# Chunked delta rule ahead of a routed feed-forward: the substitution looks one row ahead, V is scaled into PSUM, T lies in runs of 32, and two banks are read as one

## The chip, the core and the metric

The kernel runs on one NeuronCore of a Trainium2 chip. The metric is the time of one execution on the device in microseconds; lower is better. TensorE (PE) multiplies and transposes, VectorE (DVE) and ScalarE (ACT) work element by element on SBUF and PSUM, GpSimd (POOL) and SyncE (SP) mostly issue DMAs. Each engine runs its instructions in the order in which they stand; between engines, and between instructions of VectorE that depend on each other, semaphores make one wait for another.

## The reference

```python
# attention: B=4, H=8, S=768, D=48
k_n = k / (norm(k) + 1e-6)
state = zeros(B, H, D, D)
for t in range(S):
    y[:, :, t] = q[:, :, t] @ state
    v_old = k_n[:, :, t] @ state
    state += beta_t * outer(k_n[:, :, t], v[:, :, t] - v_old)
x = y.transpose(0, 2, 1, 3).reshape(B * S, H * D)      # 3072 x 384
# feed-forward: 8 experts of 384 -> 1024 -> 384
e = token_ids * 2654435761 % 8
out[e == i] = relu(x[e == i] @ w1[i]) @ w2[i]
```

All of it is in f32.

## The kernel before

The sequence is cut into 24 chunks of 32 tokens (C = 32, NU = 24), in 6 groups of 4 (GC, NG). Batch and token of the chunk lie on the 128 partitions (4 x 32), the 8 heads in the free dimension. Within a chunk the recurrence is solved in closed form. The products of keys with keys and queries with keys ("gram", L358) give a triangular system per head; its inverse T is found on VectorE by substitution; and then the chunk needs the following steps, written by `chunk(c)`:

- *ask*: keys and queries times the state S (L502, TensorE), into bank A (keys) and bank Y (queries).
- R = V1 − A (L525, VectorE, two halves). V1 is V times a factor per token (`scale_v`, L424, VectorE).
- *solve*: T times R into bank B (L536), 32 matmuls of 64x64 weights; the weights are read out of the tile Tz, in which T for two halves of the partitions lies with zeros between.
- W, a copy of bank B (L546, ScalarE, two halves).
- *update*: keys times W, added to the state in `psS` (L557); S is copied out by ScalarE (L632, two copies), for the last chunks the second one by VectorE (L630).
- *answer*: W with the masked query products MT (L584) on top of bank Y; `x_sb` is the copy of Y (L592), which GpSimd scatters to `x_scratch` in DRAM (L597).

Beside these steps a chunk prepares one that comes 8 or 9 later: *turn* transposes Q and K on TensorE (L321, into bank A for Q, Z and B for K) and ScalarE copies them to KQ (L330); *gram* goes into banks Z and B, and from there GK (keys with keys, L373, ScalarE) and GQ (queries with keys times a mask, L382, VectorE). ScalarE makes MT from GQ (L400). Chunks 0 and 2 do a second turn and gram, and the preparation ends with chunk 13.

One inverse serves a group of four chunks. VectorE transposes the keys' products (L439), and then runs 31 steps of two ops each, a product of the rows found so far with one column of the system (`tmp`, L476) and its addition to the rows left (U, L474):

```python
for j in range(C - 1):
    task("DVE", ns, (f"U{i}", row), ("tmp",), lambda j=j: step(j, False))
    task("DVE", ns, ("tmp",), (f"U{i}",), lambda j=j: step(j, True))
```

Last, a 128x1024 transpose puts T into TU (L485), and `spread_t` copies TU into Tz, by ScalarE for the first two groups (L410), by four DMAs of GpSimd's queue with runs of 4 KB for the others (L417).

The order of the work on each engine is written out: every step is a `task` with an engine, an estimated duration and names that it reads and writes, and `order()` runs through all tasks once and gives each engine the ready task with the longest rest of a chain behind it. TensorE and SyncE keep the order in which the tasks are made. LAG holds the estimated delay from one engine to the next, and a task may be put behind another that will soon be ready, within .35 of its own duration.

Then x is read back sorted by expert, and the feed-forward follows on TensorE (L993, L1023). The many small operations that count tokens per expert (`routing`) run on VectorE in the attention's time.

## Time and profile before

| what | us |
|---|---|
| median of 3 runs | 544.59 (543.64 to 547.6) |
| the profiled execution | 547.66 |
| its span, first to last instruction | 546.1 |
| TensorE busy | 474.7 (87%) |
| VectorE busy | 265.9 (49%) |
| ScalarE busy | 152.8 (28%) |
| GpSimd busy | 148.6 (27%) |
| first solve starts | 51.45 |
| second solve starts | 68.36 |
| solve of chunk 14 starts, the first without preparation | 194.58 |
| last solve starts | 265.76 |
| the experts' work begins and ends | 280.68, 538.33 |

A chunk's period is told here from one solve's start to the next. The shares are those of the whole span; the stages have different limits, so the busy times of the stretches between these marks say more than they do. 1.56 us of the profiled execution lie outside the span. The clock columns show how much of TensorE's full rate was granted, as a share of 2.4 GHz.

### The profile page before, as it was taken

Reading aid. Unit: us, or ns where it says so; the run is one execution under the profiler, and the core shown is the slowest. Engines: PE = TensorE matmul, PEld = TensorE weight load, DVE = VectorE, ACT = ScalarE, POOL = GpSimd, SP = SyncE. Lnnn points to the kernel's source line nnn. Section 1 sums busy time; section 2 is a strip of 40 time slices with the busy share of each in tenths; the row PEclk is TensorE's granted clock in tenths of the full one; section 3 lists DMA queues with packets and bytes.
Section 4 is the critical chain, followed back from the end, with each engine's and each line's share of the span. In section 5 each row is a group of like instructions: output and inputs, shape, how many; then the busy total and the mean of one; then the engine's idle time right before and its main releaser. Section 6 shows DMA issues by size and latency. Waiting matters only on the chain. (4 is left out here: it accounts for less than half of the span.)

```text
span 546.1 us, 16071 instructions
## 1 busy us (share of the span) xinstructions
PE 474.7 (87%) x6756; PEld 357.2 (65%) x6756; DVE 265.9 (49%) x764; ACT 152.8 (28%) x353; POOL 148.6 (27%) x195
## 2 busy tenths in 40 slices
PE   4874697998999888768549999999999999999993
PEld 3754586887888777667425756657576676768651
DVE  8799889899878989942111311212121221212100
ACT  3633666666455544523201000010100001010100
POOL 9400000013021032121100045071623517070621
PEclk9875878799678787988859999999999999999997
DMA  6745554446442132290099190451808145010000
GB/s 127 126 80 128 101 96 90 81 103 126 94 102 60 36 87 54 57 295 33 32 232 331 50 297 29 126 190 26 286 15 256 63 116 199 4 37 5 30 25 27
DMA packets 104345, 58.03 MB, mean 106 GB/s; under 512 B 90902, under 2 KB 99553, under 8 KB 103376
## 3 DMA queue, kind: packets, MB, share of 16 engines
q1 hardware_dynamic: 94000, 43.40, 31.9%
q0 software_dynamic: 5888, 12.53, 7.1%
q10 hardware_dynamic: 4384, 1.06, 1.1%
q8 instruction: 54, 0.88, 0.7%
q14 instruction: 19, 0.16, 0.1%
HBM read 44.51 MB, written 10.65 MB: 101 GB/s over the span
## 5 line engine op out<-in xcount | busy, mean ns | idle before, releaser
L993 PE MATMUL h_ps<-xT,w_sb 128*128 128x424 f32 (+3 forms) x384 | 130.3, 500 | 11.3 <-DMA xr<-x_scratch 11.3
L1030 POOL DMA_INDIRECT out_dram<-o_sb,idx x90 | 87.3, 970 | 160.4 <-DVE o_sb L1025 119.3
L993 PEld LDWEIGHTS h_ps<-xT,w_sb 128*128 128x128 f32 x384 | 74.3, 194 | 65.4 <-issue 28.1
L1023 PE MATMUL o_ps<-h_sb,w_sb 128*128 128x424 f32 (+3 forms) x336 | 112.3, 494 | 0.0
L1023 PEld LDWEIGHTS o_ps<-h_sb,w_sb 128*128 128x128 f32 x336 | 84.4, 251 | 27.2 <-issue 0.3
L996 ACT ACTIVATE h_sb<-h_ps 128x424 f32<-128x424 f32 (+3 forms) x32 | 15.9, 496 | 233.9 <-PE h_ps L993 209.0
L998 DVE TENSOR_SCALAR h_sb<-h_ps 128x424 f32<-128x424 f32 (+3 forms) x32 | 18.1, 565 | 113.5 <-PE h_ps L993 97.1
L597 POOL DMA_INDIRECT x_scratch<-x_sb,slot x24 | 25.1, 1047 | 160.0 <-ACT MT L400 93.5
L474 DVE TENSOR_TENSOR U<-U,tmp 128x31 f32<-128x31 f32 (+15 forms) x186 | 63.9, 343 | 5.8
L476 DVE TENSOR_TENSOR tmp<-U,Ni 128x31 f32<-128x31 f32 (+15 forms) x186 | 63.5, 342 | 5.5
L502 PE MATMUL bank<-S,KQ 128*32 128x96 f32 x1472 | 44.4, 277 | 13.4 <-ACT x_sb L592 5.2
L536 PE MATMUL bank<-R,Tz 64*64 64x48 f32 x736 | 46.3, 279 | 10.5 <-DVE R L525 7.0
L1025 DVE STREAM_TRANSPOSE o_sb<-o_ps 128x384 f32<-128x384 f32 (+2 forms) x21 | 15.5, 740 | 80.1 <-PE o_ps L1023 80.1
L536 PEld LDWEIGHTS bank<-R,Tz 64*64 64x64 f32 x736 | 43.2, 200 | 15.5 <-ACT GK L373 5.9
L502 PEld LDWEIGHTS bank<-S,KQ 128*32 128x32 f32 x1472 | 36.8, 125 | 17.8 <-ACT x_sb L592 6.5
L632 ACT ACTIVATE S<-psS 48x768 f32<-48x768 f32 x43 | 34.6, 805 | 20.7 <-PE psS L557 20.2
L557 PE MATMUL psS<-W,K 32*112 32x96 f32 x736 | 30.0, 313 | 4.9 <-ACT W L546 3.9
L584 PE MATMUL bank<-W,MT 64*64 64x48 f32 x768 | 32.1, 241 | 0.5 <-ACT W L546 0.5
L584 PEld LDWEIGHTS bank<-W,MT 64*64 64x64 f32 x768 | 28.9, 156 | 4.7 <-issue 3.4
L557 PEld LDWEIGHTS psS<-W,K 32*112 32x112 f32 x736 | 25.6, 214 | 9.2 <-ACT W L546 8.0
L330 ACT ACTIVATE KQ<-bank 128x256 f32<-128x256 f32 (+1 forms) x55 | 26.6, 487 | 16.8 <-DVE GQ L382 8.1
L546 ACT ACTIVATE W<-bank 128x192 f32<-128x192 f32 x48 | 13.2, 328 | 60.2 <-PE bank L536 57.4
(123 smaller groups left out, 403.2 us busy)
## 6 DMA issues: line engine op xcount, KB each, us to landing
w_sb<-in_moe_w_dram SPq DMA_DIRECT2D x14, 1536.0 KB
K<-in_k_dram SPq DMA_DIRECT2D x92, 48.0 KB
Q<-in_q_dram SPq DMA_DIRECT2D x88, 48.0 KB
V<-in_v_dram SPq DMA_DIRECT2D x80, 48.0 KB
xr<-x_scratch SPq DMA_DIRECT2D x16, 145.5 KB
Tz<-TU POOLq DMA_DIRECT2D x16, 128.0 KB
w_sb<-in_moe_w_dram SPq DMA_DIRECT2D x3, 512.0 KB
w_sb<-in_moe_w_dram SPq DMA_DIRECT2D x4, 384.0 KB
```

What stands on the lines that cost most here:

```text
L330: lambda bank=bank, at=at, us=us, m=m: nc.scalar.activation(KQ[:, us[0]:us[0] + m, a, :], bank[:, at:at + P * m].rearrange("p (u x) -> p u ...
L474: nc.vector.tensor_tensor(U[:, n:, 0:n], U[:, n:, 0:n], t, op=ALU.add)
L476: nc.vector.tensor_tensor(t, U[:, j:n, 0:n].to_broadcast([P, m, n]), Ni[:, j, n:, None].to_broadcast([P, m, n]), op=ALU.mult)
L502: nc.tensor.matmul(res[quarter(b), u], lhsT=KQ[:, u, a, quarter(b)], rhs=S0[:, b, u].rearrange("p r d -> p (r d)"), start=(u == 0), stop=True,
L536: nc.tensor.matmul(pw[rows, h], lhsT=Tz[rows, :, :, x0 + h].rearrange("p e i -> p (e i)"), rhs=R[rows, h], start=(h == 0), stop=True, skip ...
L557: nc.tensor.matmul(psS[0][0:DP + D, b, 2 * D * u:2 * D * u + 2 * D], lhsT=K4[quarter(b), u].rearrange("p r d -> p (r d)")[:, 0:DP + D], rh ...
L584: nc.tensor.matmul(py[rows, h], lhsT=MT[rows, h].rearrange("p e i -> p (e i)"), rhs=W[rows, h], start=(c == 0 and h == 0), stop=True, skip ...
L597: put = nc.gpsimd.indirect_dma_start(out=x_dram[:, :], out_offset=bass.IndirectOffsetOnAxis(ap=slot[:, c:c + 1], axis=0), in_=x_sb.rearran ...
L632: nc.scalar.activation(S1[half(r), :, :, r], new[half(r), :, :, r], ACT.Copy)
L993: nc.tensor.matmul(h_ps[:, :width], lhsT=w1_sb[:, co, fo * P:(fo + 1) * P], rhs=xT[:, co, :width], start=(co == 0), stop=(co == CO - 1))
L1023: nc.tensor.matmul(os_ps[i][:, 0:width], lhsT=w2_sb[:, fo, i::CO], rhs=h_sb[:, fo, 0:width], start=(fo == 0), stop=(fo == FO - 1))
L1030: scat = nc.gpsimd.indirect_dma_start(out=out_q, out_offset=bass.IndirectOffsetOnAxis(ap=idx[e][:, k:k + 1], axis=0), in_=o_sb[:, k], in_o ...
```

## The change

- **Look-ahead.** A step of the substitution is three ops in place of two: the product for the rows beyond the next (L511), the next row by itself in one op (`row`, L507), and the addition for the rows beyond it (L515). The product of step j+1 needs the row of step j, and not its addition. There are two `Ni` and four `tmp`.
- **V and R.** `scale_v` writes its product into bank A (L447), and the keys' ask adds to it there (`start=False` for the keys); W is copied with a factor of −1, so the state in `psS` is negative, and so is the sign of x_sb's copy. R is then a copy of bank A by ScalarE (L574): one of 128x384 in the chunks up to 13, two halves after. W likewise (L596). There are two R, and no V1. One matmul with zeros (L918) opens bank A.
- **T in runs.** Tz and TU hold the 32 elements of a row of T side by side, so the solve (L585) reads 64 weights in a row. The transpose into TU writes with a stride (L535). The first chunk of each group goes to Tz by ScalarE (L434), as do all four in the first two groups; the other three chunks by GpSimd's DMAs, in runs of 128 bytes.
- **Pairs.** Banks Z and B are one tile, `pair`. The copy GK (L384), the mask GQ (L388) and the copy of the turned keys (L341) are one op each on both. The turn of Q goes into bank Z.
- **Order.** Estimated durations and delays are other numbers (LAG of ScalarE 90 for 85, of VectorE 122 for 65; ops of the substitution are not put behind a coming task, but for those of the first one, for which the share is 2.0). The answer stands ahead of the turn of K. The last part of the routing's small operations is made after the last inverse (`routing_tail`).

```diff
-        bank_z, bank_a, bank_b, bank_y = tiles(4, "bank", [P, BANK], ps)
+        bank_a, bank_y = tiles(2, "bank", [P, BANK], ps)
+        pair = ps.tile([P, 2, BANK], F32, name="pair")
+        bank_z, bank_b = pair[:, 0], pair[:, 1]
...
-        Tzs = tiles(2, "Tz", [P, 2, C, NX])
-        TUs = tiles(2, "TU", [P, C, NX])
+        Tzs = tiles(2, "Tz", [P, NX, 2, C])
+        TUs = tiles(2, "TU", [P, NX, C])
...
-        LAG = {"PE": 255, "ACT": 85, "DVE": 65, "POOL": 150, "SP": 0}
+        LAG = {"PE": 255, "ACT": 90, "DVE": 122, "POOL": 150, "SP": 0}
...
+            def wait_for(i):
+                return {"inv": 0.0, "inv0": 2.0}.get(tasks[i]["kind"], 0.35)
...
+                if paired:
+                    task("ACT", 500, names, (f"GK{g % 3}{cc}0", f"GK{g % 3}{cc}1"),
+                         lambda: nc.scalar.activation(
+                             GK[:, :, cc].rearrange("p j u r -> p r u j"), both[:, :, :, 0],
+                             ACT.Copy))
+                    task("DVE", 340, names, (f"GQ{c % NGQ}0", f"GQ{c % NGQ}1"),
+                         lambda: nc.vector.tensor_tensor(
+                             GQ.rearrange("p u r y -> p r u y"), both[:, :, :, 1],
+                             mask[:, None, None, :].to_broadcast([P, 2, HU, C]),
+                             op=ALU.mult), boost=4000)
+                    return
...
+            near = GC if g < 2 else 1
+            for cc in range(near):
+                xs_ = slice(H * cc, H * cc + H)
+                for e in range(2):
+                    task("ACT", 450, (f"TU{g % 2}",), (f"Tz{g % 2}{cc}{e}", f"Tz{g % 2}{cc}{e}+"),
+                         lambda e=e, xs_=xs_: nc.scalar.activation(
+                             Tz[:, xs_, e], TU[:, xs_], ACT.Copy, scale=kmask[:, e:e + 1]))
+            for b in range(B if near < GC else 0):
+                x0 = H * near
+                task("POOL", 800, (f"TU{g % 2}",),
+                     [f"Tz{g % 2}{cc}{b % 2}" + "+" * (b // 2) for cc in range(near, GC)],
+                     lambda b=b, x0=x0: nc.gpsimd.dma_start(
+                         out=Tz[quarter(b), x0:, b % 2], in_=TU[quarter(b), x0:]), kb=150)
...
+            task("DVE", 470, four(f"v{c % 4}_") + (f"ntok{g % 3}",), ("A",),
+                 lambda: nc.vector.tensor_tensor(
+                     bank_a[:, 0:H * D].rearrange("p (h d) -> p h d", h=H), Vs[c % 4],
+                     n[:, :, None].to_broadcast([P, H, D]), op=ALU.mult))
...
+            def ahead(j, what):
+                n, m = j + 1, C - 2 - j
+                t = tmps[2 * i + j % 2][:, 0:n * m].rearrange("p (m n) -> p m n", n=n)
+                if what == "row":
+                    nc.vector.scalar_tensor_tensor(
+                        out=U[:, n, 0:n], in0=U[:, j, 0:n], scalar=Ni[:, j, n:n + 1],
+                        in1=U[:, n, 0:n], op0=ALU.mult, op1=ALU.add)
+                elif what == "mult":
+                    nc.vector.tensor_tensor(t, U[:, j:n, 0:n].to_broadcast([P, m, n]),
+                                            Ni[:, j, n + 1:, None].to_broadcast([P, m, n]),
+                                            op=ALU.mult)
+                else:
+                    nc.vector.tensor_tensor(U[:, n + 1:, 0:n], U[:, n + 1:, 0:n], t, op=ALU.add)
...
-            task("DVE", 1200, (f"U{i}",), (f"TU{i}",), lambda: nc.vector.transpose(
-                TUs[i], U))
+            task("DVE", 1860, (f"U{i}",) + (tuple(rows) if g in EAGER else ()), (f"TU{i}",), lambda: nc.vector.transpose(
+                TUs[i].rearrange("p x i -> p i x"), U))
...
-                                     start=(u == 0), stop=True,
+                                     start=(a == 1 and u == 0), stop=True,
...
+            for hs in ((range(H),) if busy else hheads):
+                part = slice(D * hs.start, D * hs.stop)
+                task("ACT", 490 if busy else 305, ("A",), [f"R{c % 2}{x}" for x in range(2)
+                                              if hheads[x].start in hs],
+                     lambda part=part: nc.scalar.activation(
+                         R.rearrange("p h d -> p (h d)")[:, part], flat_a[:, part], ACT.Copy))
...
-                        nc.tensor.matmul(pw[rows, h], lhsT=Tz[rows, :, :, x0 + h].rearrange("p e i -> p (e i)"),
+                        nc.tensor.matmul(pw[rows, h], lhsT=Tz[rows, x0 + h].rearrange("p e i -> p (e i)"),
...
-                         W[:, hs.start:hs.stop], pw[:, hs.start:hs.stop], ACT.Copy))
+                         W[:, hs.start:hs.stop], pw[:, hs.start:hs.stop], ACT.Copy, scale=-1.0))
...
-                turn(turned, 1, [("A", bank_a, 0, range(HU))])
+                turn(turned, 1, [("Z", bank_z, 0, range(HU))])
```

The first place is TensorE in one chunk with preparation, from the turn of K to the next one's products. In the names, `bank_161` is Z, `bank_162` A, `bank_163` B and `bank_164` Y; after, `bank_164` is A and `bank_165` Y. Before:

```order
L321 MATMUL bank_161<-ident,K_80 128x128 x2
L321 MATMUL bank_163<-ident,K_80 128x128 x2
L584 MATMUL bank_164<-W_107,MT_138 64x48 x16
L502 MATMUL bank_162<-S_97,KQ_116 32x96 x16
L502 MATMUL bank_164<-S_97,KQ_116 32x96 x16
L536 MATMUL bank_163<-R_105,Tz_140 64x48 x16
L321 MATMUL bank_162<-ident,Q_94 128x128 x4
L557 MATMUL psS<-W_106,K_84 112x96 x16
L358 MATMUL bank_161<-KQ_114 32x64 x4
L358 MATMUL bank_163<-KQ_114 32x64 x4
```

After:

```order
L632 MATMUL bank_165<-W_106,MT_137 64x48 x16
L331 MATMUL pair<-ident,K_84 128x128 x4
L552 MATMUL bank_164<-S_97,KQ_119 32x96 x16
L552 MATMUL bank_165<-S_97,KQ_119 32x96 x16
L585 MATMUL pair<-R_103,Tz_138 64x48 x16
L331 MATMUL pair<-ident,Q_93 128x128 x4
L607 MATMUL psS<-W_105,K_88 112x96 x16
L368 MATMUL pair<-KQ_117 32x64 x32
L632 MATMUL bank_165<-W_105,MT_136 64x48 x16
L331 MATMUL pair<-ident,K_85 128x128 x4
```

The answer has moved ahead of the turn of K, the solve's weights come from the new Tz, and the products go to the pair in one piece of 32 matmuls where before they went to the two banks in turns of 4.

The second place is VectorE in the middle of a substitution. Before, with the masks of two banks, R and a V product among the steps:

```order
L474 TENSOR_TENSOR U_148<-U_148,tmp 128x15x17
L476 TENSOR_TENSOR tmp<-U_148,Ni 128x252
L382 TENSOR_TENSOR GQ_135<-bank_163,mask 128x4x32
L382 TENSOR_TENSOR GQ_135<-bank_161,mask 128x4x32
L474 TENSOR_TENSOR U_148<-U_148,tmp 128x14x18
L476 TENSOR_TENSOR tmp<-U_148,Ni 128x247
L474 TENSOR_TENSOR U_148<-U_148,tmp 128x13x19
L476 TENSOR_TENSOR tmp<-U_148,Ni 128x240
L525 TENSOR_TENSOR R_105<-V_103,bank_162 128x192 x2
L474 TENSOR_TENSOR U_148<-U_148,tmp 128x12x20
L424 TENSOR_TENSOR V_104<-V_102,ntok_143 128x384
L476 TENSOR_TENSOR tmp<-U_148,Ni 128x231
```

After, with one mask and a V product into bank A:

```order
L507 SCALAR_TENSOR_TENSOR U_147<-U_147,Ni_149 128x13
L515 TENSOR_TENSOR U_147<-U_147,tmp_152 128x18x13
L511 TENSOR_TENSOR tmp_153<-U_147,Ni_149 128x238
L388 TENSOR_TENSOR GQ_133<-pair,mask 128x2x4x32
L507 SCALAR_TENSOR_TENSOR U_147<-U_147,Ni_149 128x14
L515 TENSOR_TENSOR U_147<-U_147,tmp_153 128x17x14
L511 TENSOR_TENSOR tmp_152<-U_147,Ni_149 128x240
L507 SCALAR_TENSOR_TENSOR U_147<-U_147,Ni_149 128x15
L515 TENSOR_TENSOR U_147<-U_147,tmp_152 128x16x15
L511 TENSOR_TENSOR tmp_153<-U_147,Ni_149 128x240
L447 TENSOR_TENSOR bank_164<-V_101,ntok_142 128x384
L507 SCALAR_TENSOR_TENSOR U_147<-U_147,Ni_149 128x16
```

A step has become three ops, in which `tmp` changes between two tiles and no op reads what the one just ahead of it wrote; R is gone from this engine.

The third place is ScalarE over one chunk with preparation. Before:

```order
L400 ACTIVATE MT_138<-GQ_128,kmask 128x8x32 x2
L546 ACTIVATE W_106<-bank_163 128x192 x2
L330 ACTIVATE KQ_110<-bank_162 128x4x128
L632 ACTIVATE S_98<-psS 48x16x48 x2
L330 ACTIVATE KQ_110<-bank_161 128x2x128
L330 ACTIVATE KQ_110<-bank_163 128x2x128
L373 ACTIVATE GK_124<-bank_161 128x4x32
L373 ACTIVATE GK_124<-bank_163 128x4x32
L592 ACTIVATE x_sb_108<-bank_164 128x4x96
L400 ACTIVATE MT_137<-GQ_129,kmask 128x8x32 x2
```

After, from one R to the next:

```order
L574 ACTIVATE R_104<-bank_164 128x384
L424 ACTIVATE MT_136<-GQ_134,kmask 128x8x32 x2
L596 ACTIVATE W_106<-pair 128x384
L341 ACTIVATE KQ_117<-pair 128x4x128
L691 ACTIVATE S_97<-psS 48x16x48 x2
L643 ACTIVATE x_sb_108<-bank_165 128x4x96
L341 ACTIVATE KQ_117<-pair 128x4x128
L384 ACTIVATE GK_122<-pair 128x2x4x32
L574 ACTIVATE R_103<-bank_164 128x384
```

R stands behind the copies of x, K and GK of the chunk before and ahead of the masks MT; W, the K copy and GK are one op each.

## Rows read from the trace of the kernel before

**Rows 1.** Windows by stage: length, busy us (instructions) of each engine, granted clock, DMA.
```profile
51.45:68.36 16.91, 11.55 (x306) 9.79 (x305) 14.23 (x61) 10.46 (x28) 1.35 (x2) 0.80 0.50 97
68.36:194.58 126.22, 116.59 (x3080) 101.33 (x3080) 111.06 (x339) 74.05 (x176) 20.12 (x33) 0.81 0.42 87
194.58:265.76 71.18, 56.62 (x1444) 50.75 (x1440) 46.45 (x139) 27.92 (x59) 16.49 (x27) 0.90 0.35 100
265.76:280.68 14.92, 3.12 (x66) 2.90 (x65) 1.75 (x7) 1.04 (x3) 1.76 (x3) 0.63 0.57 98
280.68:538.33 257.65, 255.84 (x768) 167.51 (x768) 47.90 (x85) 16.84 (x34) 90.22 (x93) 0.99 0.38 119
```

**Rows 2.** Windows by chunk, the same columns.
```profile
101.95:109.66 7.71, 7.58 (x237) 6.67 (x233) 7.33 (x21) 5.04 (x13) 0.28 (x1) 0.96 0.38 85
117.91:126.43 8.52, 7.61 (x233) 6.58 (x233) 8.04 (x26) 5.02 (x13) 3.07 (x7) 1.00 0.58 123
126.43:135.49 9.06, 7.64 (x236) 6.58 (x232) 8.27 (x31) 6.10 (x14) 1.83 (x3) 1.00 0.63 128
135.49:146.99 11.50, 11.50 (x232) 10.10 (x232) 9.66 (x28) 5.19 (x12) 2.13 (x4) 0.55 0.51 101
194.58:201.36 6.78, 5.54 (x164) 5.05 (x160) 6.40 (x20) 3.57 (x8) 1.39 (x3) 0.99 0.13 43
250.18:258.03 7.85, 6.18 (x160) 5.31 (x160) 2.13 (x5) 2.64 (x6) 1.40 (x4) 1.00 0.11 42
```

**Rows 3.** Groups of instructions, 101.95 to 109.66, weight loads of solve and answer.
```profile
L536 PEld LDWEIGHTS bank<-R,Tz 64*64 64x64 f32 x33 | 2.0, 199 | 0.6 <-issue 0.6
L584 PEld LDWEIGHTS bank<-W,MT 64*64 64x64 f32 x32 | 1.0, 135 | 0.2 <-issue 0.2
```

**Rows 4.** Groups of instructions, 135.49 to 146.99, the same two.
```profile
L536 PEld LDWEIGHTS bank<-R,Tz 64*64 64x64 f32 x32 | 1.9, 200 | 0.6 <-issue 0.6
L584 PEld LDWEIGHTS bank<-W,MT 64*64 64x64 f32 x32 | 1.8, 220 | 0.3 <-issue 0.3
```

**Rows 5.** Timeline of VectorE, 121 to 160: start, duration, instruction, idle before.
```profile
121.57 1.25 DVE L485 STREAM_TRANSPOSE TU<-U 128x1024 f32<-128x1024 f32 x1
...
145.91 0.62 DVE L525 TENSOR_TENSOR R<-V,bank 128x192 f32<-128x192 f32 x2 [0.89 <-PE bank L502]
...
149.14 0.40 DVE L476 TENSOR_TENSOR tmp<-U,Ni 128x231 f32<-128x231 f32 x1
149.57 0.40 DVE L474 TENSOR_TENSOR U<-U,tmp 128x231 f32<-128x231 f32 x1
149.89 0.55 DVE L424 TENSOR_TENSOR V<-V,ntok 128x384 f32<-128x384 f32 x1
...
152.80 0.49 DVE L382 TENSOR_TENSOR GQ<-bank,mask 128x128 f32<-128x128 f32 x2 [0.43 <-ACT KQ L330]
...
158.28 1.25 DVE L485 STREAM_TRANSPOSE TU<-U 128x1024 f32<-128x1024 f32 x1
```

**Rows 6.** Groups by shape, whole span: busy, mean ns, idle before and its releasers.
```profile
L536 PE MATMUL bank<-R,Tz 64*64 64x48 f32 x736 | 46.3, 279 | 10.5 <-DVE R L525 7.0 <-issue 1.6 <-DMA Tz<-TU 1.4
L632 ACT ACTIVATE S<-psS 48x768 f32<-48x768 f32 x43 | 34.6, 805 | 20.7 <-PE psS L557 20.2
L525 DVE TENSOR_TENSOR R<-V,bank 128x192 f32<-128x192 f32 x46 | 14.1, 349 | 10.4 <-PE bank L502 10.4
L592 ACT ACTIVATE x_sb<-bank 128x384 f32<-128x384 f32 x24 | 11.9, 496 | 6.0 <-PE bank L584 2.8 <-ACT GK L373 1.7 <-issue 1.1
L330 ACT ACTIVATE KQ<-bank 128x256 f32<-128x256 f32 x30 | 11.7, 397 | 8.9 <-DVE GQ L382 8.1 <-PE bank L321 0.8
```

**Rows 7.** Timeline at the start, VectorE, ScalarE and TensorE.
```profile
21.70 0.19 DVE L476 TENSOR_TENSOR tmp<-U,Ni 128x31 f32<-128x31 f32 x1
...
46.95 0.51 ACT L410 ACTIVATE Tz<-TU,kmask 128x256 f32<-128x256 f32 x1 [8.17 <-DVE TU L485]
...
68.36 0.90 PE L536 MATMUL bank<-R,Tz 64*64 64x48 f32 x12 [3.57 <-DVE R L525]
```

More of the change, by code (lines that the diff above doesn't have):

```diff
@@ L120 @@
         LEAD, AHEAD, MORE = 8, 9, (0, 2)
+        EAGER = range(NG)
         SPLIT = NU - GC
@@ new lines, in inverse @@
+            for j in range(C - 1 if g in EAGER else 0):
+                n, row = j + 1, f"Ni{i}_{0 if j < L else L}"
+                rows = [f"U{i}r{x}" for x in range(C)]
+                ns = 70 + 1.04 * n * (C - 2 - j)
+                if n < C - 1:
+                    task("DVE", ns, (f"U{i}", rows[j], row), (f"tmp{2 * i + j % 2}",),
+                         lambda j=j: ahead(j, "mult"), kind="inv0" if g == 0 else "inv")
+                task("DVE", 70 + 1.04 * n, (f"U{i}", rows[j], row), (rows[n],),
+                     lambda j=j: ahead(j, "row"), kind="inv0" if g == 0 else "inv")
+                if n < C - 1:
+                    task("DVE", ns, (f"U{i}", f"tmp{2 * i + j % 2}"), rows[n + 1:],
+                         lambda j=j: ahead(j, "add"), kind="inv0" if g == 0 else "inv")
@@ L635 @@
         slot = st.tile([P, NTC], I32)
[L637 removed]
+        registers_later, routing_tail = [], []
         def routing():
@@ L798, in registers @@
+            routing_tail.append(tail)
             def registers():
```

263 lines of the change are left out of this document (129 added, 134 removed).

## The prediction

> **What bounds the kernel now.** I read the windows by stretch first, because the bound changes between stages [rows 1]. The expert stage, 257.65 us, has TensorE busy for 255.84 us; the change leaves it alone, and also the 14.92 us gap before it. All that can move lies in the 265.76 us before. In the 13 chunk periods from 68.36 to 194.58 TensorE is busy 116.59 of 126.22 us and VectorE 111.06, so both are close to the bound; ScalarE has 74.05.
>
> The windows by chunk show what kind of bound it is [rows 2]. A period with the clock at full level takes 7.71 or 9.06 us, with 7.58 and 7.64 us of TensorE work. The one at 135.49 has a granted clock of .55, that is mostly the lower level (1.2 of 2.4 GHz), and takes 11.50 us, all of it TensorE; of the 13, five have a clock of .64 or less and take 9.5 to 11.5. So there are two limits: a chunk at the lower clock is TensorE's alone, and a fast one is shared with VectorE. VectorE's own limit shows in its timeline [rows 5]: the transpose that closes one inverse starts at 121.57, the next at 158.28. Four chunks take 36.71 us, and the waits seen there are of a few tenths (.89 for keys, .43 for ScalarE). I take 34.9 us of it as work and hand-over from op to op, 8.7 us per chunk, an estimate.
>
> **Solve.** The weights' reading order is changed, from a stride of 32 elements to 64 in a row. The answer has the same 64x64 weights, already in a row. At full clock, 32 weight loads of the solve take 2.0 us and 32 of the answer 1.0 us [rows 3]; at the lower clock they take 1.9 and 1.8 [rows 4]. The solve is thus held by its weight reads at the full clock and by the clock otherwise. I take −.85 us per chunk at full clock (between 0, if the stride is not the cause, and −1.0) and −.1 per one at the lower clock. TensorE's fast chunk goes from 7.58 to about 6.75.
>
> The Trainium skill, "SBUF — State Buffer", section of the cachelines, says that reads which cross into a new 16-byte line each time pay a penalty; the two weight-load rows agree at full clock, and no rule there separates the lower clock, where the rows show no penalty.
>
> **Substitution.** Before, each op waits for the one just ahead of it. In [rows 5], 149.14 + .40 ends at 149.54 and the next begins at 149.57: +.03. The independent V product begins at 149.89 while its neighbour runs until 149.97: −.08. After the change every op waits for the op two ahead, so two hand-overs per step gain .12 us between them (the third op, one row, takes the place of a hand-over: from .08 before the product ends to about the product's end, if it takes .19 as the smallest op does [rows 7]). An op costs .16 + 1.04 us per 1000 elements (231 elements .40, 384 .55). The ops that remain on the path have 9920 elements in all instead of 10912, −1.0 us. Thirty steps x .12 = 3.6, plus 1.0, plus .2 for the last step: −4.8 us per inverse. Bounds: −1.0 with no overlap of hand-overs and a free row, +5.8 if nothing overlaps (a rival below).
>
> **R and V.** Two VectorE ops in .62 us [rows 5] go away per chunk; ScalarE gets one copy of 128x384, which costs .50 as the copy of x does [rows 6]. V's product stays, but writes PSUM; no row shows this, and I take the .55 of now, between .45 and .75. It must now wait until ScalarE has read R of the chunk before from the same bank, and on VectorE the steps of the substitution stand behind it; ScalarE read it most of a period earlier, so I price that wait at nothing, and at up to .5 us per chunk if the V product comes early in the order. ScalarE's load at 5.04 us of a period [rows 2] becomes at most 5.5, below the rest. What can hurt is its order: R stands behind x, K and GK copies, and the solve waits for R. One period along ScalarE, an estimate: R .5, solve 1.0 and hand-over .35, W .5, update and hand-over 1.25, S 2 x .805, then x .5 and two copies of like size at .55, 6.8 us by the rows of the x and S copies [rows 6] and the 1.0 of the weight loads [rows 3]. It fits under the 7.3 found below, with little to spare.
>
> **Paired banks, row products.** Two masks in .49 [rows 5] become one of 256, .43 by the line above: −.06 to −.1 us per chunk on VectorE. The merged copies on ScalarE save two or three tenths, hidden.
>
> **T's layout.** The closing transpose writes with a stride; 1.25 us now, bounds 1.25 and 2.0, and I take 1.6: +.35 per inverse. For the last four groups three chunks in four come by GpSimd's DMAs in 128-byte pieces instead of 4 KB. Now this transfer is waited for once, 1.4 us [rows 6]. After, the first chunk of a group comes from ScalarE, and the others have a period more; I price it at −1.4 to +4 (the last groups), taking 0.
>
> The Trainium skill, "DMA: Bandwidth & Descriptors", Specifications, asks for 512 bytes for line rate, a rule against this part; its section on small descriptors excepts transfers within the chip's own memory. By the first the upper end, +4, would be the one to take.
>
> **Moved work.** The tail of the routing, some 40 small ops of about .2 us, stands on VectorE behind the last transpose, where a period has 2.13 us of VectorE work in 7.85 [rows 2]; 8 us over the last three periods fit, and only a state copy can find one ahead of it: nothing, at most +.6 in all. Before it left, it lay between the steps of the substitution; what that gives back I leave in the rounding. The answer ahead of the K turns on TensorE only exchanges neighbours in a row of work, and the one product that clears bank A falls into the wait for the first T. GpSimd still issues four transfers per group. Priced at nothing, all three.
>
> **Sum.** VectorE per four chunks: 34.9 − 4.8 − 2.5 − .3 + .35 = 27.7, or 6.9 per chunk. TensorE 6.75. Hand-overs such as the .1 to 1.4 us that separate TensorE's work from the period now add up to about .4 on top of the larger one: 7.3 us per fast busy chunk.
>
> - *Until the first solve.* The first substitution runs from 21.70 to the transpose that ScalarE waits 8.17 us for at 46.95 [rows 7]; TensorE can do little in that time. −4.8 + .35 = −4.4 (−1 to −5).
> - *First solve to second, 16.91 us.* TensorE waits 3.57 us for R, which stands in VectorE's queue [rows 7]. With R on ScalarE that goes, and .85 of the solve; something of it returns behind ScalarE's own queue. −4 (−1 to −6).
> - *13 busy periods, 126.22 us.* 13 x 7.3 = 95, plus 2.6 for a period that carries a second set of turns and products, plus periods at the lower clock. Of those there are now five; the idle on TensorE per period stays about the same (.5), so I expect two or three still, each +4. 95 + 2.6 + 10 = 107.5: −19 (−8 with five at the lower clock, −28 with none).
> - *9 late periods, 71.18 us.* No turns and products: a fast one takes 6.78 us with 5.54 of TensorE [rows 2], a chain from keys to R, solve, W, update and state. Shorter by .85 in seven, by the 1.4 us wait for T, and by about half of the 3.4 us that solves wait for R besides the 3.57 [rows 6, 7]: −6 − 1.4 − 1.7 = −9 (−4 to −13).
>
> Total −36.4. The profiled execution took 547.66 us, 3.1 over the median of 544.59, so 511.3 on its base and 508.2 on the median's; I say 509. A measurement of this kernel can tell about 1% from no change.
>
> **Rivals.**
> 1. *The clock takes the gain.* Less work per chunk means more idle on TensorE, and each period at the lower clock gives nothing back for the solve: 11.4 us. For: the period before the one at .55 in [rows 2] has only 1.42 us of idle in all. Against: the one before that has .91 and the clock stayed full. With eight such periods of the 13, 95 + 2.6 + 33 = 130 and no gain there, late ones −4: 544.6 − 4.4 − 4 + 4 − 4 = 536. With five, −8 there and −7 late: 524, the likelier form.
> 2. *ScalarE's order is the bound.* R behind copies that in turn wait for VectorE's masks: if .7 us more per period over 22 periods, +15: 524. For: ScalarE's copies of K already wait 8.1 us for VectorE's masks [rows 6], and the estimate of 6.8 is close to 7.3. Against: it is busy for 5.04 of 7.71 us.
> 3. *The layout isn't the cause.* The solve stays at 2.0: 16 fast chunks x .85 lost, +14: 523. Against: [rows 3] with [rows 4], where the same form differs by layout alone.
> 4. *Slower: VectorE takes its ops strictly one after the other.* Then 31 row ops x .22 = 6.8 are added, less 1.0 of elements: +5.8 per inverse instead of −4.8. Per four chunks 34.9 + 5.8 − 2.5 + .05 = 38.3, 9.6 a chunk; with hand-overs 10.0, over the 9.7 that the 13 periods average now. It decides from about +4 us per inverse on. Start +6, first period +1, 13 x 10.0 + 2.6 = 133, +6, late −2: 555. Against: in [rows 5] two R ops of .349 each [rows 6] lie within .62, and V overlaps both neighbours.
>
> The Trainium skill, "VectorE: DVE Perf Modes", section "The DRAIN you can't avoid", states this fourth rule: the next op does not start until the pipe is empty, with or without semaphores between. The trace agrees only for ops that wait for each other, and its own next section lets an op that is not held start earlier.
>
> **How the numbers follow.** Forecast .57 (498 to 519); rival 1 .15, rival 2 .10, rival 3 .07 (all 520 to 537); a loss and gain that cancel, within 1% of 544.6, .06; rival 4 .05. Faster by over 1% .89, within .06, slower .05. The range for 8 in 10: up to 534, which takes in the likelier forms of rivals 1 to 3, and down to 495, where none of the busy periods falls to the lower clock and the late chain gives −13.
>
> **What the profile after would show.** Solve weight loads near 140 ns mean against 200 now; row, add and product with starts that overlap, an inverse of about 18.6 us undisturbed against 23.4; the first solve near 47; no solve that waits for VectorE, but some that wait for ScalarE's R; fast busy periods near 7.3, and those at the lower clock still near 11.4. The prediction is wrong if the periods at the lower clock number under one or over four in the 13, if R's wait on ScalarE passes .7 us per chunk, or if the last groups' T arrives after its chunk asks for it.

## The result

The changed kernel takes 519.68 us (median of 4, 519.3 to 523.05) against 545.84 before: a ratio of .9536 (95% interval .9479 to .9593), 4.6% faster. Forecast were 509 us and a range of 495 to 534. The range holds; the middle was 11 us too hopeful. Of the experiments' executions three of e2, two of e3 and one of e9 took over 1.5% more than the shortest of their kernel, and without these their medians are 541.7, 539.9 and 543.4 us, which the text compares.

The windows by stage, profiled execution of after (span 517.7 us), same columns as [rows 1]. Busy periods are those of the chunks that still prepare another one, late periods those after; one busy period carries a second set of turns and products:

```profile
0.00:47.53 47.53, 33.08 (x1102) 25.34 (x1102) 42.39 (x173) 23.66 (x59) 18.81 (x37) 0.81 0.58 106
47.53:68.73 21.20, 14.44 (x304) 12.00 (x305) 15.82 (x70) 11.46 (x24) 1.47 (x3) 0.54 0.56 119
68.73:178.15 109.42, 92.83 (x3080) 79.12 (x3080) 93.81 (x366) 77.54 (x149) 22.16 (x33) 0.97 0.49 97
178.15:240.12 61.97, 47.33 (x1444) 41.33 (x1440) 45.41 (x181) 35.12 (x84) 18.31 (x28) 0.94 0.43 114
```

| stretch | before | after | moved | forecast |
|---|---|---|---|---|
| until the first solve | 51.45 | 47.53 | −3.9 | −4.4 |
| first solve to second | 16.91 | 21.20 | +4.3 | −4 |
| 13 busy periods | 126.22 | 109.42 | −16.8 | −19 |
| 9 late periods | 71.18 | 61.97 | −9.2 | −9 |
| last solve to the experts | 14.92 | 13.85 | −1.1 | 0 |
| experts to the end | 265.4 | 263.7 | −1.7 | 0 |

Before, the last two rows are 280.68 − 265.76 and 546.1 − 280.68; after, 253.97 − 240.12 and 517.7 − 253.97. The rows sum to the 28.4 us by which the span fell. Five of six agree with the forecast within 2.2 us; the second row has the wrong sign and is, with 8 us, the whole miss.

Inside the busy stretch things went another way than forecast, though the sum is near. Two of its periods and a late one, to lay beside [rows 2]:

```profile
107.16:115.10 7.94, 6.83 (x233) 5.84 (x233) 7.25 (x34) 5.40 (x11) 1.70 (x3) 1.00 0.45 93
139.01:147.03 8.02, 6.96 (x233) 6.01 (x233) 7.65 (x37) 5.36 (x11) 1.05 (x1) 1.00 0.48 97
191.03:197.48 6.45, 4.97 (x164) 4.39 (x160) 6.04 (x24) 4.39 (x12) 1.32 (x3) 1.00 0.42 93
```

A busy period at full clock takes 7.8 to 8.4 us (7.12 the last), not 7.3, with 6.7 to 7.2 of TensorE and mostly 7.1 to 7.7 of VectorE in it: neither engine fills it. On the other side, no busy period of this execution is at the lower clock, apart from the one with the second set (14.21 us at .77), where five were at .64 or less. The 16.8 us split so: the 12 periods with one set took 8.53 on average before where the clock was .96 or more (7 of them) and take 7.93 now, 7.1 us; five at the lower clock were together 11.4 us longer than five of the seven's mean; the period with two sets grew by 1.65. In these two executions, then, most of what the busy stretch gave is the clock.

What fills the 8.0 us is seen on two engines. TensorE over one chunk of after, start, duration, operation and idle before:

```profile
139.01 1.20 PE L585 MATMUL pair<-R,Tz 64*64 64x48 f32 x32 [0.41 <-ACT R L574]
140.15 0.66 PE L331 MATMUL pair<-ident,Q 128*128 128x128 f32 x4
141.44 0.75 PE L607 MATMUL psS<-W,K 32*112 32x96 f32 x20 [0.64 <-ACT W L596]
```

and ScalarE over the same chunk:

```profile
140.90 0.49 ACT L596 ACTIVATE W<-pair 128x384 f32<-128x384 f32 x1 [1.15 <-PE pair L331]
142.69 1.63 ACT L691 ACTIVATE S<-psS 48x768 f32<-48x768 f32 x2 [0.81 <-PE psS L607]
145.49 0.60 ACT L341 ACTIVATE KQ<-pair 128x512 f32<-128x512 f32 x1 [0.57 <-DVE GQ L388]
145.98 0.61 ACT L384 ACTIVATE GK<-pair 128x256 f32<-128x256 f32 x1
146.38 0.53 ACT L574 ACTIVATE R<-bank 128x384 f32<-128x384 f32 x1
```

The solve ends at 140.21, yet W starts only at 140.90, when the turn of Q (140.15 to 140.81) is over, and the update waits for W. W reads bank B, the turn writes bank Z: different banks, one tile `pair`. From the K copy (145.49), which had waited .57 for the mask, to R (146.38) ScalarE has no gap: K, GK, R, then the solve. So I read the period as the round R, solve, turn, W, update, S, x, K, GK; e6 tests the turn's part of it. TensorE's work is not far below: 6.96 of the 8.02 us, and the .64 that it waits for W and .42 ahead of the next solve are all of its idle time.

The groups by shape of after (busy, mean ns, idle before):

```profile
L585 PEld LDWEIGHTS pair<-R,Tz 64*64 64x64 f32 x768 | 27.3, 142 | 15.5 <-ACT R L574 7.6 <-issue 4.4 <-ACT GK L384 2.4
L535 DVE STREAM_TRANSPOSE TU<-U 128x1024 f32<-128x1024 f32 x6 | 11.7, 1957 | 0.1
L447 DVE TENSOR_TENSOR bank<-V,ntok 128x384 f32<-128x384 f32 x24 | 13.6, 569 | 8.6 <-ACT R L574 7.6 <-issue 0.9
L596 ACT ACTIVATE W<-pair 128x384 f32<-128x384 f32 x14 | 6.9, 491 | 15.1 <-PE pair L331 14.0 <-PE pair L585 1.1
```

The solve's weight loads take 142 ns against 200 before, the closing transpose 1.96 us against 1.25, V into PSUM .57 against .55 and waits 7.6 us in all for R's copy. W waited 14.0 us for the turn, the time included in which the solve ran. And the look-ahead on VectorE, product, row and addition:

```profile
140.09 0.37 DVE L515 TENSOR_TENSOR U<-U,tmp 128x220 f32<-128x220 f32 x1
140.39 0.36 DVE L511 TENSOR_TENSOR tmp<-U,Ni 128x210 f32<-128x210 f32 x1
140.68 0.23 DVE L507 SCALAR_TENSOR_TENSOR U<-U,Ni 128x21 f32<-128x21 f32 x1
140.83 0.36 DVE L515 TENSOR_TENSOR U<-U,tmp 128x210 f32<-128x210 f32 x1
141.12 0.35 DVE L511 TENSOR_TENSOR tmp<-U,Ni 128x198 f32<-128x198 f32 x1
```

The product starts .07 before the addition ends, the row .07 before the product ends, the addition .08 before the row ends. The Trainium skill's "VectorE: DVE Perf Modes", "The DRAIN you can't avoid", says that the next op does not start until the pipe empties, and that an op which is not held starts earlier; for ops that don't wait for one another these rows agree with the second, as the forecast took from [rows 5].

### The profile page after: what moved, and what is told of

Its sections match the earlier page's. It is cut to its first block, busy times and chain, and to the rows that moved or that the text cites. A ratio compares the mean times of both kernels' runs of the same rounds, so it can differ in the third digit from the quotient of the medians.

```text
span 517.7 us, 16220 instructions
## 1 busy us (share of the span) xinstructions
PE 444.8 (86%) x6758; PEld 326.9 (63%) x6758; DVE 246.9 (48%) x876; ACT 165.8 (32%) x350; POOL 152.8 (30%) x196
## 3 DMA queue, kind: packets, MB, share of 16 engines
q10 hardware_dynamic: 4384, 1.06, 1.1%
## 5 line engine op out<-in xcount | busy, mean ns | idle before, releaser
L1061 PE MATMUL h_ps<-xT,w_sb 128*128 128x424 f32 (+3 forms) x384 | 129.4, 497 | 11.1 <-DMA xr<-x_scratch 11.1
L515 DVE TENSOR_TENSOR U<-U,tmp 128x30 f32<-128x30 f32 (+9 forms) x180 | 58.0, 322 | 0.0
L511 DVE TENSOR_TENSOR tmp<-U,Ni 128x30 f32<-128x30 f32 (+9 forms) x180 | 57.7, 321 | 0.1
L507 DVE SCALAR_TENSOR_TENSOR U<-U,Ni 128x1 f32<-128x1 f32 (+30 forms) x186 | 42.0, 226 | 0.2
L585 PE MATMUL pair<-R,Tz 64*64 64x48 f32 x768 | 31.1, 228 | 8.6 <-ACT R L574 4.9
L585 PEld LDWEIGHTS pair<-R,Tz 64*64 64x64 f32 x768 | 27.3, 142 | 15.5 <-ACT R L574 7.6
L607 PE MATMUL psS<-W,K 32*112 32x96 f32 x736 | 24.7, 272 | 13.1 <-ACT W L596 13.1
L607 PEld LDWEIGHTS psS<-W,K 32*112 32x112 f32 x736 | 20.9, 178 | 17.5 <-ACT W L596 17.4
L632 PE MATMUL bank<-W,MT 64*64 64x48 f32 x768 | 28.7, 225 | 2.4 <-issue 1.9
L632 PEld LDWEIGHTS bank<-W,MT 64*64 64x64 f32 x768 | 25.5, 139 | 4.8 <-issue 2.1
L368 PE MATMUL pair<-KQ 48*32 48x64 f32 (+1 forms) x1248 | 20.8, 237 | 8.0 <-ACT KQ L341 5.6
```

The source lines that it names most:

```text
L507: nc.vector.scalar_tensor_tensor(out=U[:, n, 0:n], in0=U[:, j, 0:n], scalar=Ni[:, j, n:n + 1], in1=U[:, n, 0:n], op0=ALU.mult, op1=ALU.add)
L511: nc.vector.tensor_tensor(t, U[:, j:n, 0:n].to_broadcast([P, m, n]), Ni[:, j, n + 1:, None].to_broadcast([P, m, n]), op=ALU.mult)
L515: nc.vector.tensor_tensor(U[:, n + 1:, 0:n], U[:, n + 1:, 0:n], t, op=ALU.add)
L585: nc.tensor.matmul(pw[rows, h], lhsT=Tz[rows, x0 + h].rearrange("p e i -> p (e i)"), rhs=R[rows, h], start=(h == 0), stop=True, skip_group ...
L607: nc.tensor.matmul(psS[0][0:DP + D, b, 2 * D * u:2 * D * u + 2 * D], lhsT=K4[quarter(b), u].rearrange("p r d -> p (r d)")[:, 0:DP + D], rh ...
L632: nc.tensor.matmul(py[rows, h], lhsT=MT[rows, h].rearrange("p e i -> p (e i)"), rhs=W[rows, h], start=(c == 0 and h == 0), stop=True, skip ...
```

## The experiments

All but e9 are edits of the changed kernel. Each ran beside the kernel before on the same chip, and its ratio is to that; as not all ran on one chip, ratios compare better than times. The times are medians of all executions. The base of the table is e5, the changed kernel itself once more. "The planner" is `order()`.

| run | what | us | ratio, 95% |
|---|---|---|---|
| e1 | no look-ahead, first substitution without priority | 528.97 | .9740 (.9688 to .9792) |
| e2 | old layout of T | 543.17 | .9993 (.9958 to 1.0029) |
| e3 | turn of Q ahead of the solve | 540.65 | .9958 (.9919 to .9997) |
| e4 | second turn of Q in bank A | 518.76 | .9574 (.9498 to .9650) |
| e5 | the change again | 516.39 | .9479 (.9428 to .9529) |
| e6 | two tiles for Z and B | 507.48 | .9343 (.9277 to .9410) |
| e7 | no look-ahead, priority kept | 519.87 | .9540 (.9477 to .9602) |
| e8 | R copied by VectorE | 519.72 | .9562 (.9493 to .9630) |
| e9 | before, with T in runs alone | 543.73 | .9943 (.9908 to .9978) |
| e10 | two tiles, no look-ahead | 516.05 | .9453 (.9406 to .9500) |
| e11 | two tiles, second sets in chunks 1 and 3 | 510.62 | .9335 (.9289 to .9381) |
| e12 | two tiles, turn of Q ahead of the solve | 512.96 | .9435 (.9381 to .9488) |

**e1 and e7, the look-ahead undone.**

```diff
-        EAGER = range(NG)
+        EAGER = ()
```

> The changed kernel with the two-op steps of the substitution put back (62 dependent ops per inverse), all else as changed. Theory 1, that ScalarE's round R, solve, W, S, x, K, GK sets the busy periods at 8.0 us and VectorE has about .6 us to spare in each: the first solve comes 4 us later, a busy period grows from 8.0 to about 8.5, the late ones hardly; 528 to 533 us. Theory 2, that VectorE itself sets the busy periods: every 4.8 us per inverse is paid, 1.2 per chunk over 17 chunks and 4 at the start; 540 to 545 us. If the overlap of VectorE's ops gives nothing, about 520.

The time, 529, was theory 1's, but not the reason: the first solve came at 61.14, since the two-op steps didn't have the first substitution's priority in the planner. From the second solve on it was no slower. So once more, with that priority (`kind="inv0" if g == 0 else "inv"`):

> The changed kernel with the two-op steps, and with the first substitution ahead of other work on VectorE as the change has it (the run before lost it: its first solve came at 61.1 us). First solve near 51.5 (47.5 with look-ahead); busy periods 7.9 to 8.0 as in the run before, since VectorE does not set them; 521 to 525 us. If the look-ahead is worth its 4.8 us in every inverse: 540.

519.87: 3.5 us slower than e5, by intervals that overlap, and as fast as the run of the result (.9540 against .9536): the look-ahead is worth 0 to 3.5 us here, less than forecast. The first solve is at 50.34 (48.08 in e5). The windows, first period and a busy one, and the solve that follows the last chunk of a group:

```profile
50.34:66.38 16.04, 13.04 (x304) 10.75 (x305) 11.34 (x44) 10.42 (x23) 2.11 (x3) 0.57 0.57 120
140.36:148.30 7.94, 6.73 (x232) 5.81 (x233) 6.50 (x16) 5.28 (x11) 1.18 (x2) 1.00 0.53 105
132.26 1.14 PE L585 MATMUL pair<-R,Tz 64*64 64x48 f32 x32 [1.37 <-ACT Tz L434]
```

Most busy periods without look-ahead are 7.8 to 8.1 us, as with it: VectorE doesn't set those. It sets the ones that end a group: there the solve waited 1.00, 1.37 and 1.36 us for the group's T, and the periods are 9.44, 8.87 and 8.66. And the first period is 16.04, where the look-ahead has 21.2.

**e2, the old layout of T** (Tz, TU, `spread_t`, the transpose and the solve's weights as before):

```diff
-        lhsT=Tz[rows, x0 + h].rearrange("p e i -> p (e i)"),
+        lhsT=Tz[rows, :, :, x0 + h].rearrange("p e i -> p (e i)"),
```

> The changed kernel with T in its old layout: weights of the solve read with a stride of 32, closing transpose contiguous (1.25 us), Tz by ScalarE for two groups and by four full DMAs for the others. Theory 1 (the solve lies in ScalarE's round between R and W): .85 us more per chunk at full clock, some 20 chunks, less .7 at the start; 533 to 538 us, with weight loads of about 200 ns. Rival, that TensorE's idle time of about 1 us per period hides the solve: 520 to 524 us. Whether the periods at the lower clock come back is open; each would add 3.5 us.

541.7 is over every theory: of the change's gain some 2 us are left. A busy period, a late one, and the weight loads:

```profile
175.56:184.41 8.85, 7.56 (x232) 6.65 (x232) 7.09 (x27) 5.37 (x11) 1.88 (x3) 1.00 0.20 48
214.42:221.19 6.77, 5.53 (x164) 5.04 (x160) 6.16 (x26) 4.00 (x11) 1.18 (x3) 1.00 0.27 62
L585 PEld LDWEIGHTS pair<-R,Tz 64*64 64x64 f32 x768 | 44.5, 200 | 12.6 <-ACT R L574 10.8 <-issue 0.3
```

Typically 8.8 against 7.9 in e5 (the nine busy periods at full clock are 8.87 on average, 7.92 in e5), 6.77 against 5.94: .83 to .95 us per chunk, the size forecast. Over some 20 chunks at full clock this is about 17 us of the 25 by which the medians differ. The profiled execution of e2 was its shortest (537.2 us), with three busy periods at a clock of .65 to .69; its others went up to 548.3, and what they had more of, no profile shows.

**e9, T in runs of 32 alone, in the kernel before** (the same lines the other way round).

> The kernel before with T in runs of 32 alone (new Tz and TU, strided closing transpose of 1.96 us, first chunk of a group by ScalarE, the rest by DMA in 128-byte runs). If the solve's weight reads are worth .85 us wherever the solve is on the path: the late periods go from 7.0 to about 6.2, and the busy ones at full clock, where VectorE is the bound with 8.3 to 9 us, gain nothing or lose .2 (the longer transpose): 533 to 538 us. If most of the change's 27 us comes from this part: 520 to 526. Periods at the lower clock are expected to stay, since they gain .1 each.

543.4 against 546.14: a gain of .5 to .6%, less than forecast. One wait (us in total, times, longest) and the groups by shape, solve and ask:

```profile
ACT KQ L330 <- DVE GQ L382: 22.0, 13, 4.2
L535 PEld LDWEIGHTS bank<-R,Tz 64*64 64x64 f32 x736 | 28.2, 153 | 17.5 <-DVE R L524 8.4 <-ACT GK L373 5.6 <-issue 1.8
L535 PE MATMUL bank<-R,Tz 64*64 64x48 f32 x736 | 31.8, 239 | 11.9 <-DVE R L524 11.3 <-issue 0.2
L501 PE MATMUL bank<-S,KQ 128*32 128x96 f32 x1472 | 46.2, 285 | 21.4 <-ACT x_sb L591 13.3 <-ACT S L631 3.8 <-DVE S L629 1.8
```

The weight loads fell from 200 to 153 ns and TensorE's solve from 279 to 239, but the waits grew: for R from 7.0 us to 11.3, for x_sb's copy from 5.2 to 13.3. That copy stands on ScalarE behind K's, and K's copies now wait 22.0 us for VectorE's masks (8.1 before, as the prediction quotes it). The gain in the solve is there, and TensorE spends it waiting for VectorE's R and for copies behind VectorE's masks; five busy periods stayed at a clock of .68 or less, and the late ones, expected at 6.2, took 6.0 to 8.9. Alone the part is worth 2 to 3 us, with the rest of the change around it 22 to 25.

**e3 and e12, the turn of Q ahead of the solve** (its four lines moved up in `chunk`).

> The changed kernel with the turn of Q ahead of the solve on TensorE, where it stood behind it. In the trace W starts .7 us after the solve's end and is released by the turn of Q, which writes the other bank of the pair. Theory 1: W's wait for the turn is in the round that sets the period; it goes, the solve may start .2 to .3 later; -.3 to -.5 us per busy period, 13 of them: 513 to 516 us. Rival, that VectorE or TensorE sets the period: 518 to 521 us. Rival, that the turn now delays the solve by its whole .66: 522 to 525 us.

All theories missed: 539.9, 20 us slower. One chunk of it, TensorE and then ScalarE:

```profile
126.25 0.67 PE L589 MATMUL pair<-R,Tz 64*64 64x48 f32 x16
127.61 0.67 PE L589 MATMUL pair<-R,Tz 64*64 64x48 f32 x16 [0.70 <-ACT KQ L341]
126.96 0.60 ACT L341 ACTIVATE KQ<-pair 128x512 f32<-128x512 f32 x1 [0.88 <-PE pair L589]
```

W is now released by the solve, as theory 1 had it. But the solve breaks in the middle for .70 us, waiting for the copy of the turned Q, and that copy has waited .88 for the first half of the solve. The copy reads bank Z, the solve writes bank B. So the periods at full clock are 8.3 to 8.6 us, half a microsecond longer, and seven of the 13 fell to a clock of .69 and took 11 us, three longer: those seven are nearly the whole loss. With two tiles:

> Two tiles for Z and B, and the turn of Q ahead of the solve, the order that cost 21 us with the pair. Theory 1, that there the copy of the turned Q (bank Z) and the solve's second half (bank B) waited for each other only because both banks are one tile: with two tiles the order costs little, at most the .66 us of the turn ahead of the solve in some periods; 506 to 514 us, no solve that waits for the copy of KQ. Rival, that the order itself puts .7 us into every solve: 525 us or more.

512.96. In the waits no solve waits for KQ, and W waits for the solve alone (us in total, times, longest):

```profile
ACT W L602 <- PE bank L591: 9.4, 12, 1.9
```

The same order costs 20 to 24 us with the pair and 5 without it, and no busy period is at the lower clock. In what is left, TensorE has nothing to do between the solve and the update, and waits .6 to .9 us for W in each period.

**e6, two tiles** (`unpaired`; GK, GQ and the K copy are two ops each again).

```diff
-        pair = ps.tile([P, 2, BANK], F32, name="pair")
-        bank_z, bank_b = pair[:, 0], pair[:, 1]
+        bank_z, bank_b = tiles(2, "bank", [P, BANK], ps)
```

> The changed kernel with banks Z and B as two tiles again and two ops each for GK, GQ and the copies of K; the turn of Q stays in bank Z behind the solve. Theory 1: two tiles end the waits between the turn of Q and W, which touch different banks: W starts about .2 us after the solve's end in place of .7, and a busy period at full clock is 7.5 to 7.7 us in place of 8.0, less what the extra ops cost in ScalarE's round (up to .3). 514 to 519 us with the clock full. Rival, that the wait is for the work and not for the tile: W stays released by the turn, 8.0 to 8.3, 520 to 524 us. A period at the lower clock would add 2 to 3 us each to either, and would show.

507.48, the fastest of all, 1.4% under e5 by the ratios, with intervals that just miss each other. Two busy periods, and W:

```profile
131.64:139.00 7.36, 6.72 (x232) 5.81 (x232) 7.36 (x33) 5.38 (x14) 1.40 (x3) 1.00 0.54 115
101.72:109.09 7.37, 6.75 (x232) 5.83 (x233) 7.37 (x31) 6.21 (x15) 1.97 (x4) 1.00 0.44 92
L598 ACT ACTIVATE W<-bank 128x384 f32<-128x384 f32 x14 | 6.9, 491 | 8.9 <-PE bank L587 8.9
```

W is released by the solve, and TensorE's wait of .64 for W is gone from all busy periods but the last. The twelve with one set take 7.46 us on average, and in nine of them VectorE is busy for all but .1 us: this comes near the 7.3 that the forecast had named. The planner, on its own, also put R ahead of GK's copies in this version, so the .5 us is not all the wait of W.

**e10, two tiles and no look-ahead.**

> Two tiles for Z and B (as in the run at 507.5 us), and the two-op steps of the substitution. Theory: in that kernel VectorE is busy for the whole of most busy periods, 7.4 us, so there the look-ahead counts: +1.2 us per chunk in 12 chunks or so, where the pair had hidden it, and 3 us at the start; 518 to 524 us. Rival, that something else sets those 7.4 us: 510 to 512 us, the start alone.

516.05, 8.6 us slower than e6, between theory and rival and nearer to theory; the intervals touch. Two of its busy periods:

```profile
113.65:122.42 8.77, 7.18 (x233) 6.00 (x233) 8.66 (x33) 7.56 (x18) 2.22 (x4) 1.00 0.50 113
132.59:141.27 8.68, 6.93 (x232) 5.91 (x232) 8.13 (x22) 5.40 (x14) 1.32 (x2) 1.00 0.54 108
```

They are 8.7 us with VectorE busy for 8.1 to 8.7, others 7.1 to 7.5; the eleven at full clock are 7.83 on average, .37 longer than in e6, where the theory had 1.2, so VectorE alone doesn't set the 7.4. By the medians the look-ahead is worth 8.6 us here against 0 to 3.5 with the pair. But of the 10.7 us between the profiled executions only 4.3 lie in the busy stretch and 7.3 in the late one, where some periods of e10 are at a lower clock or have gaps that stay open (see e5), and the time up to the second solve gives back .7; how much of the 8.6 is the look-ahead's own is not shown.

**e4, the second turn of Q in bank A.** This run leaves out a matmul with zeros that would open bank A again after the turn, so its sums are not those of the kernel, and its time stands for the work and its order alone. The edit also puts V's product behind the turn.

```diff
-                    turn(turned, 1, [("Z", bank_z, 0, range(HU))])
+                    turn(turned, 1, [("A", bank_a, 0, range(HU))])
+                    scale_v(c + 1)
```

> The changed kernel, but in chunks 0 and 2 the second turn of Q goes into bank A, as before the change, and V is scaled into A behind it. Theory 1: the first period is 21.2 us (16.9 before) because that turn waits for the copies out of bank Z (1.80 us) and the products after it for its own copy (2.97 us); without these two waits it is 16.5 to 17.5, and 514 to 516 us in all. Rival, that the second mask's place in VectorE's queue sets the second solve: the first period stays at 20 to 21 us, 518 to 520 in all.

The first period is 20.73 us (21.20), as the rival had it. TensorE in it:

```profile
59.17 1.18 PE L368 MATMUL pair<-KQ 48*32 48x64 f32 x64 [0.61 <-ACT GK L384]
65.95 2.79 PE L552 MATMUL bank<-S,KQ 128*32 128x96 f32 x64 [4.55 <-DVE bank L447]
```

The two waits went (.61 is left) and one of 4.55 took their place, for V, which stands among the steps of the substitution in VectorE's queue. As the edit itself put V there, the run doesn't tell what the period would be without the two waits alone, and it was V and not the rival's mask that was waited for.

**e11, the second sets in chunks 1 and 3** (`MORE = (1, 3)`, two tiles).

> Two tiles for Z and B, and the second turn and product of a period in chunks 1 and 3 where it was in 0 and 2. Theory, that the first period (19 us) is long because its second set of products waits for copies behind ScalarE's other work, and R then waits for that set's mask: the first period 12 to 14 us, the second 10 to 12 where it was 7.4; 503 to 506 us. Rival, that VectorE's inverse sets the first periods whatever stands in them: 506 to 509 us.

The first two periods were 11.50 and 15.81 us, 27.3 together, against 19.12 and 7.38, 26.5, and the first four 45.5 against 47.3. By their ratios e11 and e6 are equal. The second set took its time with it, and nothing was gained. The first period is even shorter than the theory's 12 to 14 us, the second longer than its 10 to 12; the rival's reason did not show either, for VectorE is busy in only 3.78 of the first period's 11.50 us.

**e8, R copied by VectorE** (`nc.vector.tensor_copy`, one op in the chunks up to 13).

> The changed kernel with the copy of R by VectorE in the chunks up to 13 (one op of 128x384), by ScalarE in the rest. Theory 1, ScalarE's round sets the period: R no longer stands behind K's and GK's copies; 7.4 to 7.7 us per busy period, 512 to 516 us with the clock full. Rival, that VectorE is then the bound (7.1 to 7.5 busy of 8.0 now, plus .5) or that R waits there behind masks and steps: 8.0 to 8.3, 519 to 524 us.

519.72: nothing gained. Its busy periods are 7.6 to 8.4 (6.87 the last). W still waits for the turn (14.4 us in all), TensorE is idle ahead of the solves for 8.3 us in all, 8.6 in the changed kernel, and the first period grew to 22.70.

**e5, the change again.**

> The changed kernel itself once more, as the base for the runs beside it. 517 to 522 us. Open is whether its late periods of 6.4 us, with gaps of .25 to .34 inside the solve that no engine explains, come again, or are 5.94 as in the three runs before; and whether all its busy periods keep the full clock, as they did.

516.39. A busy period mostly at the lower clock and a late one of its profiled execution, the longest of the six:

```profile
69.27:80.96 11.69, 11.11 (x232) 9.71 (x232) 7.65 (x31) 4.77 (x9) 1.21 (x2) 0.52 0.44 85
194.91:200.84 5.93, 4.69 (x164) 4.21 (x160) 5.87 (x24) 4.38 (x12) 1.81 (x3) 1.00 0.48 105
```

Two of the 13 busy periods and one late one were at .50 to .64 here, none of the busy ones in the first profile; the ten others with one set are 7.92 on average. The late periods are 5.94 without gaps in the solve; the 6.4 of the first profile did not come again there, in e4 and e6 most are 5.94 too, in e10 and e11 several are 6.3 to 6.4. What the gaps are stays open.

## Why the prediction was right and where it failed

- **Solve.** Right, and measured by e2: .83 to .95 us per chunk at full clock, weight loads 200 ns with the stride, 142 without. Taking it back costs most of the gain, but it gives this only in company: alone it gave 2 to 3 us (e9).
- **Substitution.** Overlap as read from [rows 5]; the first one shrank from 23.87 us (21.70 to 45.57) to 20.67 (22.59 to 43.26), with other ops between its steps in both, −3.2 for −4.8. Its share of the gain was put wrong: forecast as a term of every period, it pays 0 to 3.5 us here, since VectorE sets only the periods that end a group (e7); 8.6 in e10 against e6.
- **T's layout.** The transpose grew by .71 us, I took .35, inside the bounds. No instruction waited for the DMAs with 128-byte runs in the profile after. The Trainium skill's 512 bytes for line rate ("DMA: Bandwidth & Descriptors", Specifications) would have made the upper bound, +4 us, the one to take; no run shows them, which agrees with the exception on the same page that the forecast named.
- **R and V, the step that failed in the first period.** "With R on ScalarE that goes, and .85 of the solve": forecast −4, measured +4.3. The wait for R did shrink, from 3.57 us to 1.06. TensorE, then VectorE and ScalarE in this period of after, and last the same products and copy in e7:

```profile
59.10 1.11 PE L331 MATMUL pair<-ident,Q 128*128 128x128 f32 x4 [1.80 <-ACT GK L384]
63.19 1.18 PE L368 MATMUL pair<-KQ 48*32 48x64 f32 x64 [2.97 <-ACT KQ L341]
68.73 0.49 PE L585 MATMUL pair<-R,Tz 64*64 64x48 f32 x9 [1.06 <-ACT R L574]
66.81 0.41 DVE L388 TENSOR_TENSOR GQ<-pair,mask 128x256 f32<-128x256 f32 x1
60.02 0.89 ACT L424 ACTIVATE MT<-GQ,kmask 128x256 f32<-128x256 f32 x2
60.82 0.90 ACT L434 ACTIVATE Tz<-TU,kmask 128x256 f32<-128x256 f32 x2
61.62 1.04 ACT L459 ACTIVATE U<-zero 128x1024 f32<-128x1024 f32 x1
62.56 0.58 ACT L341 ACTIVATE KQ<-pair 128x512 f32<-128x512 f32 x1
67.25 0.60 ACT L341 ACTIVATE KQ<-pair 128x512 f32<-128x512 f32 x1 [4.12 <-DVE GQ L388]
68.14 0.54 ACT L574 ACTIVATE R<-bank 128x384 f32<-128x384 f32 x1
62.07 1.18 PE L368 MATMUL pair<-KQ 48*32 48x64 f32 x64 [0.69 <-ACT KQ L341]
61.42 0.60 ACT L341 ACTIVATE KQ<-pair 128x512 f32<-128x512 f32 x1 [0.53 <-PE pair L331]
```

  Two things took the gain. First the clock: TensorE's 304 matmuls took 14.44 us at a clock of .54, where 306 took 11.55 at .80 before, +2.9, and at this clock the solve itself saves almost nothing (1.94 us against 2.01), which the prediction's own term (−.1 at the lower clock) had said. Second, new waits for ScalarE: before, TensorE waited 1.79 us for a KQ copy here besides R; after, .93 for W, 1.80 for GK and 2.97 for a KQ copy, +3.9. With −2.5 for R that is the +4.3. The longest of them is ScalarE's own queue: the turn of Q ends at 60.21, and its copy starts at 62.56, behind copies for MT and Tz and the fill of U with zeros. In e7, where only the steps of the substitution and with them the planner's order differ, the copy follows its turn at once, TensorE waits .69, and the period is 16.04. That "something of it returns behind ScalarE's own queue" was in the forecast, but not its size. The second mask stands in VectorE's queue behind steps of the second inverse, and K's copy, GK and R behind the mask, as in rival 2; but the turn of K, which that copy needs, ends only at 65.41 and the ask, which R needs, at 67.67, so this adds half a microsecond at R at most. e7 also gives back in this period what it loses before it (second solve at 66.38, 69.27 in e5). Why the clock in this period is .50 to .57 in all the changed kernels is not shown.
- **The busy periods: two errors against each other.** The step that gave 7.3 us per busy chunk at full clock, from VectorE's work plus hand-overs, was mis-sized: 7.93, along ScalarE's round, which I had put at 6.8. The sum of that round left out the wait of W for the turn, .64 us, as I took the two banks of the pair for independent, and the .57 that K's copy waits for the mask. W's own row, e3 and e12 show that they are not; e6 shows what the period is without W's wait (and with R ahead of GK), 7.46. So the pair, priced as a small gain, cost 7 to 9 us (e6 against e5). Against that, I expected two or three periods at the lower clock at +4 each; the first profile has none, the second two. By its own sign (fewer than one such period) the prediction would be wrong after the first profile and not after the second; that the sum of this stretch came near is luck: +7.6 us in twelve periods and +4.3 in the one with two sets (14.21 for 9.9) stand against the −10 at the clock.
- **Late periods.** −9.2 for −9; what made up the −9.2 was not taken apart.
- **Rivals.** Rival 2 came in part: the round on ScalarE is longer by +.63 per busy period, but the larger piece is W behind the turn and not R behind copies; TensorE waited 7.6 us for W in the busy stretch and some 6 ahead of the solves. Rival 1 did not come in the changed kernel's busy periods, but did in e3 (seven periods); its likelier form adds up to 521 on the median's base, not 524. Rival 3 is refuted by e2, rival 4 by the rows of VectorE.

Which part of the change keeps the clock up is not settled: TensorE's idle time per busy period with one set is .9 to 1.4 us after and .1 to 1.9 before in those that kept it, so the amount alone doesn't tell the two apart, and no run held everything but the clock.

## What to carry to other kernels

A stall that is moved to another engine is gone only if the queue there leaves room: follow the new neighbours of the moved instruction and of every copy that the next stage needs, not just its own inputs (here a copy came 2.35 us after its input was ready). Two banks made one tile save instructions, and here also made a reader of one bank wait for a writer of the other; count these waits (.64 us in a round of 8) against the instructions saved. Parts of a change that relieve different engines don't add up: T in runs was worth 2 to 3 us alone and 22 to 25 in the changed kernel, the look-ahead 0 to 3.5, or 8.6 with two tiles; so the worth of a part is measured in the kernel that it will live in.
